# Order of the SP queue and of the last two units in a fused attention and two-MoE kernel

## The chip, the cores and the metric

One core of a Trainium2 chip runs the whole program. The metric is the device time of one execution in microseconds (us). An execution has five compute engines' worth of work: TensorE (PE, with its weight loads as PEld), VectorE (DVE), ScalarE (ACT), GpSimd (POOL), and SyncE (SP), which here only issues transfers. Sixteen DMA engines move the data.

## The reference

```python
x = attention(q, k, v)            # 4 x 8 heads, 576 x 64; a local band of |i-j| < 4, plus
                                  # full attention over means of 4 rows, repeated 4 times
logits = x @ phi                  # x: 2304 x 512; 32 slots, 4 for each of 8 experts
slot_in = softmax(logits, 0).T @ x
slot_out[e] = relu(slot_in[e] @ w1[e]) @ w2[e]          # 512 x 1024, 1024 x 512
x = softmax(logits, 1) @ slot_out
noisy = x @ w_gate + log1p(exp(x @ w_noise)) * noise    # second MoE: top 2 of 8 experts
out[t] += gate * (relu(x[t] @ w1[e]) @ w2[e])           # for the two experts of each row t
```

All is float32. The weights of each MoE are 32 MB.

## The kernel before

The attention is done in 16 units, each two heads of one batch. A unit needs its keys and queries (`load`, L192: four transfers of 144 KB into one of two `ld` buffers) and its values (`load_v`, L213: four transfers of 80 KB into one of three `V` buffers); all of these move in runs of 64 floats. A unit passes through some forty small blocks: A0 and A1 transpose `ld` on PE (`a_pe`, L237), S makes the local scores (`b_s`, L288 and L293), SD the coarse ones (`b_d`, L304), CP and CD turn the probabilities (L379, L390), VD makes the means of the values (`v_pe`, L274), DP and DD multiply with the values (L417, L424), EP transposes the result (L444), LG makes logits (L466), and once per batch SU adds the slots' sums (`slot_u`, L524).

The order is written out by hand. The loop `for p in range(-1, NU - 1)` (L593) walks the string `SEQ` in each step p: a name stands for one block of the unit p minus the block's offset, so a step works on four units at once: `ld` loads unit p+2, A0 and A1 are unit p+1, `lV` loads the values of unit p+1, S is unit p. What is left of the units 13 to 15 after step 14 is the string `TSEQ`, with the unit written beside each block (`S:15`). Nothing reorders it: an engine takes its instructions in the order of the text.

SP issues every load, in the order of the text too. `W` calls `flush`, which issues the next transfers of the first MoE's weights (`wr`, 512 KB each): eight weight matrices are asked for during the attention, one transfer at each `W` of the steps 1 to 12, two at each of the steps 13 and 14. The eight small loads (`small`, L598: the gate's weights and the noise, 16 KB or 4 KB each, in runs of 8 floats) are issued four at a time at the start of the steps 13 and 14. The program gives SP's transfers eight counters in turn, and an issue waits until the transfer that had its counter before has landed, so at most eight are in flight.

`R2` (`ring_2`, L630) gives the attention's buffers up and loads three more weight matrices into their place (`w8a` to `w10b`, 1 MB each), as soon as the last reader of what lay there is done: `w8a` needs unit 15's transposes, `w8b` its S, `w9a` its SD, `w9b` its DP, `w10a` its DD. Five more matrices (`wr`) go into buffers that the first MoE's products give back. The first MoE (L794 to L830) then takes the matrices in this order; its last product is `yacc`, L825.

`cp` (L223) copies a PSUM result to SBUF on ACT, or on DVE where the copy's name stands in `ON_V` (in the tail: `ON_V_END`).

Of the kernel before, what the change touches and what calls it, by code (L numbers as in the profile page):

```python
# [15 lines left out]

CAP = 640

SEQ = """ld DM S DD A0 M a00 a01 A1 W a110 XA a100 SD EL a101 ST a111 SK CP SS EX W VD EP01 MD V0 EP00 EP10 SU_ LG CD
EP11 EP V1 LA ED0 DX SU KD ED1 DP lV x1 x0 DQ1 X0 SE DQ0 RD P0 X1 P1""".split()  # L20
TSEQ = """S:15 DD:13 XA:13 DM:14 CP:14 W EP01:14 EP00:14 SD:15 M:15 EL:15 EP10:14 EX:15 EP11:14 CD:14 ED0:14 MD:15 SU:15 VD:14 DP:14 V0:14 V1:14 EP:13
ED1:14 P0:15 P1:15 DD:14 DX:15 LG:13 X0:13 RD:15 x0:14 DM:15 x1:14 CP:15 LA:13 EP00:15 X1:13 EP01:15 EP11:15
CD:15 EP10:15 XA:14 ED0:15 VD:15 DP:15 V0:15 V1:15 ED1:15 DD:15 EP:14 x0:15 x1:15 LG:14 X0:14 XA:15 LG:15 EP:15 X0:15 LA:14
LA:15 SE:3 X1:14 SK:2 H2 MT M4 X1:15 SS:3 H2 ST:3 MB R2 QW QS UA DN UB H1 SI H2 SK:3""".split()

ON_V = ['k1', 'd1', 'a101', 'a111', 'v0']
ON_V_END = ['P0', 'k1', 'v0', 'v1']

NW = [0] + [1] * 12 + [2] * 2

# [1 line left out]
NPRE = 8  # L32
NHOT = [4, 8]
N2 = 3
# [4 lines left out]
def attn_moe_moe_kernel(ctx: ExitStack, tc: tile.TileContext, q, k, v, moe_phi, moe_w1, moe_w2,  # L39
                        w_gate, w_noise, noise, w1, w2, out, dbg=None):  # L40
    nc = tc.nc
    B, H, S, D = q.shape
    NT = B * S
    DM = H * D
# [11 lines left out]
    NU = len(units)  # L56
# [21 lines left out]
    def consts():  # L78
        nc.vector.tensor_tensor(sums[:, 0], idf[:, 0:32], idf[:, 32:64], op=ALU.add)
        nc.vector.tensor_tensor(sums[:, 0], sums[:, 0], idf[:, 64:96], op=ALU.add)  # L80
        nc.vector.tensor_tensor(sums[:, 0], sums[:, 0], idf[:, 96:128], op=ALU.add)
        nc.vector.tensor_copy(sums[:, 1:4], sums[:, 0:1].to_broadcast([128, 3, 32]))
        nc.vector.tensor_reduce(out=bd, in_=idf.rearrange("p (t s) -> p t s", t=4), axis=AX.X, op=ALU.add)
# [10 lines left out]
    def wload(src, kk, pool=ringa, names=("wr", "wr")):  # L94

        n = kk // 2
        ts = [pool.tile([128, 2048], F32, name=nm).rearrange("p (k f) -> p k f", k=n) for nm in names]
        sv = src.rearrange("(k p) f -> p k f", p=128)

        def go(i, eng=nc.sync, ks=range(n), whole=0):  # L100
            if whole:
                m, k = n // 2, n // 2 * (whole - 1)
                return eng.dma_start(out=ts[i][:, k:k + m], in_=sv[:, n * i + k:n * i + k + m])
            for k in ks:
                eng.dma_start(out=ts[i][:, k:k + 1], in_=sv[:, n * i + k:n * i + k + 1])
        return lambda k: ts[k // n][:, k % n], [lambda i=i, **k: go(i, **k) for i in range(len(names))]
# [12 lines left out]
    with ExitStack() as tctx:  # L119
# [62 lines left out]
        def tp():  # L182
            return ps.tile([128, 512], F32, name="t", bufs=4)

        LD, KD, DQ, SD, SS, SB, PD, PL, XL, XT, XK = ({} for _ in range(11))
# [32 lines left out]
                    if j1 < 5:  # L218
                        nc.sync.dma_start(out=V[64:121, 4, h], in_=hv[h, S - 57:S])

        TAIL = []

        def cp(name, dst, src, alt=False):  # L223
            if name not in (ON_V_END if TAIL else ON_V) and not alt:
                nc.scalar.activation(dst, src, AF.Copy)  # L225
            else:
                nc.vector.tensor_copy(dst, src)
# [13 lines left out]
        def a_evac(u, i, h, j):  # L241
            if i:
                hs = slice(64 * h, 64 * h + 64)
                cp(f"a1{h}{j}", Q[hs, 288 * j:288 * j + 288, h], AT[u, 1, j][hs, 0:288], u == 0)
            else:
                cp(f"a0{j}", K[:, 3 + 288 * j:291 + 288 * j], AT[u, 0, j][:, 0:288])
# [51 lines left out]
        def b_d(u):  # L298
            kd = KD.pop(u)
            sd = ps.tile([128, 512], F32, name="Sd")  # L300
            if u == 1:
                hot(NHOT[1], sd)
            for qb in range(3):
                nc.tensor.matmul(sd[0:96, qb * 144:qb * 144 + 144], Dq[:, qb].rearrange("p h i -> p (h i)"), kd,  # L304
                                 start=True, stop=True, skip_group_check=True)
            SD[u] = sd

        def soft_m(u):
            m = wka.tile([128, NG], F32, name="m")
# [23 lines left out]
        def soft_p(u, a):  # L333
            El, su = PL[u]
            as_ = slice(64 * a, 64 * a + 64)
            eng = nc.vector if f"P{a}" in (ON_V_END if u == NU - 1 else ON_V) else nc.gpsimd
            eng.tensor_tensor(P[as_, :, HQ * a:HQ * a + KW], El[as_],  # L337
# [28 lines left out]
        def soft_dm(u):  # L366
            Ed, rd = PD[u]
            eng = nc.vector if "DM" in (ON_V_END if u == NU - 1 else ON_V) else nc.gpsimd
            eng.tensor_tensor(Ed, Ed, rd[:, :, None].to_broadcast([96, 3, 144]), op=ALU.mult)
# [68 lines left out]
        ET_ = {}  # L438
# [22 lines left out]

        def logit_pe(u):
            xT, kk = XT[u], u % 4
            L = SB[u + 2][:, 0:192] if not TAIL else ET_[u][1][:, 128:320] if u in ET_ else tp()[:, 0:192]
            for t in range(4):
                nc.tensor.matmul(L[32 * t:32 * t + 32, 0:128], phi[:, kk], xT[:, 128 * t:128 * t + 128],  # L466
                                 start=True, stop=True, skip_group_check=True)
            for t in range(4):
                nc.tensor.matmul(L[32 * t:32 * t + 32, 128:192], phi[:, kk], xT[:, 512:576], start=True, stop=True,
                                 skip_group_check=True)  # L470
            LL[u] = L

        def logit_add(u):
            L = LL[u]
            LT = LTs[(u // 4) % 2]
            if u % 4 == 0:
                nc.vector.tensor_copy(LT, L)
            else:
                nc.vector.tensor_tensor(LT, LT, L, op=ALU.add)

# [63 lines left out]
        def hot(n, t=None):  # L544

            t = t or ps.tile([128, 512], F32, name="S")
            for _ in range(n):
                nc.tensor.matmul(t, onesb, onesb[:, None].to_broadcast([128, 4, 128]), start=True, stop=True)

        def ok(u):  # L550
            return 0 <= u < NU
# [21 lines left out]
        MW, todo = {}, []  # L573

        def mload(i, pool, names=("wr", "wr")):
            MW[i], go = wload((moe_w1, moe_w2)[i % 2][i // 2], (4, 8)[i % 2], pool, names)
            if i == 2 * E - 1:
                go = [lambda f=f, c=c: f(ks=(c, c + 2)) for c in range(2) for f in go]
            todo.extend([lambda f=f, c=c: f(whole=c) for f in go for c in (1, 2)] if len(MW) <= NPRE else go)

        def flush(n=99):
            for _ in range(min(n, len(todo))):
                todo.pop(0)()

        for i in range(NPRE):
            mload(ORDW[i], ringa if i < 3 else ringb)
        small = [(wgn[:, :, E * i:E * i + E], w.rearrange("(k p) e -> p k e", p=128))
                 for i, w in enumerate((w_gate, w_noise))]
# [4 lines left out]
        for p in range(-1, NU - 1):  # L593
            if p == 0:
                nc.sync.dma_start(out=phi, in_=moe_phi.rearrange("(k p) s -> p k s", p=128))
            for _ in range(4 if p >= NU - 3 else 0):
                o, i = small.pop(0)
                nc.sync.dma_start(out=o, in_=i)  # L598
            if p == 1:
                nc.gpsimd.memset(zero, 0.0)  # L600
            b4, r4 = divmod(p - 5, 4)
            for nm in SEQ:
                f, off, a = BL.get(nm, (None, 99, ()))
                if off is None:
                    if 0 <= b4 < B and r4 == a:
                        f(b4)
                elif ok(p - off):
                    f(p - off, *a)
                if nm == "W" and p >= 0:
                    flush(NW[p])  # L610
                if p == -1 and nm == "lV":
                    nc.gpsimd.memset(PT, 0.0)
                    nc.gpsimd.memset(Vd[:, 1], 0.0)
                    nc.gpsimd.memset(PdT[:, 1], 0.0)
                if p == -1 and nm == "DQ1":
                    nc.vector.memset(P, 0.0)
            if p == 0:
                hot(NHOT[0])
                nc.vector.tensor_scalar(trib, jp, 0.0, None, op0=ALU.is_gt)
                consts()  # L620
# [47 lines left out]
        def slot_in():  # L668
            t = tp()
            for kk in range(4):  # L670
# [6 lines left out]
              "W": flush}  # L677
        TAIL.append(1)
        for nm in TSEQ:
            if nm in TB:  # L680
                TB[nm]()
            elif nm[0] == "H":
                hot(int(nm[1:]))
            else:
                n, u = nm.split(":")
                f, off, a = BL[n]
                f(int(u), *(a if off is not None else ()))


# [567 lines left out]
    for e in range(E):  # L1257
# [36 lines left out]
        elif nx is not None:  # L1294
# [4 lines left out]
            for n in range(NTILE):  # L1299
                i = s0 + n // 9  # L1300
# [25 lines left out]
        for sl, n0, n1 in SCAT:  # L1326
            if sl // 5 == e:
                f = fill[sl % 5]
# [9 lines left out]
    with tc.If(ov > 0):  # L1338
        with ExitStack() as octx:
# [6 lines left out]
            with tc.For_i(0, E, 1) as ei:  # L1346
# [4 lines left out]
                go = op_.tile([128, NTILE], F32, name="go")  # L1351
# [59 lines left out]
```

## Time and profile before

| | us |
|---|---|
| median of 3 runs (lowest, highest) | 491.67 (491.55, 493.74) |
| the profiled execution | 490.25 |
| its span, first to last instruction | 488.5 |
| PE busy in the span | 462.5 |
| granted clock of TensorE, mean over the span | 0.981 |

The attention with its tail fills the first 158 us, the first MoE goes on to 188 us, the routing to 207 us, and the second MoE's experts take the rest. The page cuts the span in 40 slices; a digit is the busy share of a slice in tenths, for DMA the mean share of its sixteen engines.

### The profile page before, as it was taken

What the parts mean: (1) busy time and instruction counts of PE and PEld (TensorE: products, weight loads), DVE (VectorE), ACT (ScalarE), POOL (GpSimd) and SP (SyncE); (2) the same over time, 40 slices, a digit from 0 to 9 for tenths busy, and PEclk for the clock granted to TensorE, in tenths of its full rate; (3) what the DMA queues carried; (4) which work ended last, traced back from release to release, by engine and by line L of the source; (5) the groups of instructions that cost most, each with busy time, mean ns of one, the idle gap of its engine ahead of it and who ended that gap; (6) DMA issues with size and microseconds to landing.
All of it is one profiled execution on the core that took longest, in us unless ns stands there. A gap on an engine that the chain in (4) does not pass through costs nothing.

```text
span 488.5 us, 12466 instructions
## 1 busy us (share of the span) xinstructions
PE 462.5 (95%) x4765; PEld 358.7 (73%) x4765; DVE 275.3 (56%) x703; ACT 270.5 (55%) x699; POOL 220.1 (45%) x321
## 2 busy tenths in 40 slices
PE   6999999899789999999999999999999999999992
PEld 5798788788575443577777887887887877878882
DVE  6888878878575321876578464383552634615300
ACT  2688877778483112665384464682755646727410
POOL 7898777678331001084556577322222222212232
PEclk9999999999799999979999999999999999999998
DMA  8999999999989999999977843799867855333333
GB/s 163 213 208 257 213 245 216 205 264 186 251 250 333 397 389 395 375 345 335 377 186 203 230 68 67 190 363 280 273 88 214 214 127 144 45 43 45 44 44 46
DMA packets 108233, 104.19 MB, mean 213 GB/s; under 512 B 67978, under 2 KB 77898, under 8 KB 108170
## 3 DMA queue, kind: packets, MB, share of 16 engines
q1 hardware_dynamic: 101258, 90.50, 62.5%
q0 software_dynamic: 6912, 12.85, 17.5%
q8 instruction: 40, 0.66, 0.6%
q14 instruction: 23, 0.19, 0.1%
HBM read 83.60 MB, written 19.73 MB: 212 GB/s over the span
## 4 chain that ended last, share of the span: by engine, by line
PE 58%; DMA 16%; issue 12%; SPq 3%; DVE 3%; ACT 3%; POOL 2%; POOLq 2%; ACTq 0%; DVEq 0%
PE y L1062 35%; DMA wr<-in_moe_w_dram 7%; DMA ld<-in_q_dram 5%; SPq L192 3%; PE t L237 3%; PE gx L879 2%; PE S L293 2%; PE h L1042 2%; PE Sd L304 2%; POOL out_dram L1081 2%; DMA V<-in_v_dram 2%; DMA w10b<-in_moe_w_dram 1%; POOLq L1087 1%; PE gx L1042 1%; PE xs L942 1%
## 5 line engine op out<-in xcount | busy, mean ns | idle before, releaser
L1062 PE MATMUL y<-whi,hh 128*128 128x512 f32 x320 | 127.6, 399 | 0.3 <-ACT hh L1043 0.3
L1062 PE MATMUL y<-whi,hl 128*128 128x512 f32 x320 | 127.7, 399 | 0.0
L1062 PE MATMUL y<-wlo,hh 128*128 128x512 f32 x320 | 127.3, 398 | 0.0
L1081 POOL DMA_INDIRECT out_dram<-ys,idx x40 | 63.9, 1597 | 110.3 <-ACT ys L1073 61.2
L1073 ACT ACTIVATE ys<-y,gt 128x512 f32<-128x512 f32 x40 | 27.4, 685 | 82.4 <-issue 47.1
L1062 PEld LDWEIGHTS y<-wlo,hh 128*128 128x128 f32 x320 | 60.5, 189 | 13.0 <-issue 0.8
L1034 DVE TENSOR_TENSOR wlo<-wr,whi 128x512 fp32r<-128x512 f32 x64 | 42.0, 692 | 49.5 <-ACT whi L1031 38.0
L1062 PEld LDWEIGHTS y<-whi,hh 128*128 128x128 f32 x320 | 60.7, 190 | 12.0 <-ACT hh L1043 0.6
L1062 PEld LDWEIGHTS y<-whi,hl 128*128 128x128 f32 x320 | 60.6, 189 | 11.5 <-issue 2.1
L1008 POOL DMA_INDIRECT tab<-stk,pos x36 | 35.8, 994 | 11.5 <-issue 10.4
L1044 DVE SCALAR_TENSOR_TENSOR hl<-h,hh 128x256 fp32r<-128x256 f32 (+1 forms) x64 | 31.3, 490 | 16.5 <-ACT hh L1043 14.3
L1044 DVE SCALAR_TENSOR_TENSOR hl<-gx,hh 128x256 fp32r<-128x256 f32 (+1 forms) x64 | 31.3, 488 | 11.1 <-ACT hh L1043 8.5
L1031 ACT ACTIVATE whi<-wr 128x512 fp32r<-128x512 f32 x64 | 36.9, 625 | 0.2
L1043 ACT ACTIVATE hh<-gx 128x256 fp32r<-128x256 f32 (+1 forms) x64 | 28.1, 439 | 16.0 <-PE gx L1042 13.2
L1043 ACT ACTIVATE hh<-h 128x256 fp32r<-128x256 f32 (+1 forms) x64 | 27.9, 436 | 13.5 <-PE h L1042 10.7
L237 PE MATMUL t<-idf,ld 96*128 96x96 f32 x192 | 23.5, 271 | 10.8 <-DMA ld<-in_k_dram 7.3
L1080 POOL MEMSET spacer<- 1x1 f32 x40 | 13.6, 339 | 42.4 <-issue 42.4
L255 POOL TENSOR_TENSOR s<-Q 64x288 f32<-64x288 f32 x31 | 29.3, 944 | 2.4
L237 PEld LDWEIGHTS t<-idf,ld 96*128 96x128 f32 x192 | 18.8, 154 | 15.0 <-issue 6.2
L337 POOL TENSOR_TENSOR P<-El,su 64x350 f32<-64x350 f32 x31 | 24.4, 786 | 11.3 <-DVE su L330 5.4
L225 ACT ACTIVATE PT<-t 64x384 f32<-64x384 f32 (+1 forms) x64 | 25.9, 428 | 3.1 <-PE t L379 1.9
L927 DVE TENSOR_TENSOR oh<-iot,R 128x256 fp32r<-128x256 f32 (+2 forms) x50 | 20.7, 447 | 11.5 <-PE xs L945 7.8
(312 smaller groups left out, 882.3 us busy)
## 6 DMA issues: line engine op xcount, KB each, us to landing
wr<-in_moe_w_dram SPq DMA_DIRECT2D x72, 512.0 KB
wr<-in_moe_w_dram SPq DMA_DIRECT2D x88, 256.0 KB
out_dram<-zero SPq DMA_DIRECT2D x20, 256.0 KB
V<-in_v_dram SPq DMA_DIRECT2D x62, 80.0 KB
ld<-in_k_dram SPq DMA_DIRECT2D x32, 144.0 KB
ld<-in_q_dram SPq DMA_DIRECT2D x32, 144.0 KB
XT<-tab SPq DMA_DIRECT2D x5, 320.0 KB
tab<-zero SPq DMA_DIRECT2D x6, 256.0 KB
```

What stands on the lines that cost most here:

```text
L225: nc.scalar.activation(dst, src, AF.Copy)
L237: nc.tensor.transpose(t[:, 96 * c:96 * c + 96], ld[:, i, 3 * j + c].rearrange("p h d -> p (h d)"), idf[0:96, 0:96])
L255: nc.gpsimd.tensor_tensor(q2, q4[:, :, 0:2], q4[:, :, 2:4], op=ALU.add)
L337: eng.tensor_tensor(P[as_, :, HQ * a:HQ * a + KW], El[as_], su[as_, :, None].to_broadcast([64, NG, KW]), op=ALU.mult)
L1008: st = nc.gpsimd.indirect_dma_start(out=tab, out_offset=bass.IndirectOffsetOnAxis(ap=pos[:, c, i:i + 1], axis=0), in_=stk[:, i].bitcast(F3 ...
L1031: nc.scalar.activation(whi[:, kk], wb(kk), AF.Copy)
L1034: eng.tensor_tensor(wlo[:, kk], wb(kk), whi[:, kk].bitcast(F32), op=ALU.subtract)
L1043: nc.scalar.activation(hh[:, f], h, AF.Relu)
L1044: nc.vector.scalar_tensor_tensor(hl[:, f], h, 0.0, hh[:, f].bitcast(F32), op0=ALU.max, op1=ALU.subtract)
L1062: nc.tensor.matmul(y, l[:, kk, ts_], r_[:, kk], start=(m == 0), stop=(m == 23))
L1073: nc.scalar.activation(ys, YS.pop((e, ti)), AF.Copy, scale=gt[:, ti:ti + 1])
L1081: st = nc.gpsimd.indirect_dma_start(out=out, out_offset=bass.IndirectOffsetOnAxis(ap=idx[:, ti:ti + 1], axis=0), in_=ys, in_offset=None, c ...
```

## The change

- `lV` moves from the end of `SEQ` to the place just behind A1, where the first `W` stood; that `W` moves behind CD. So in each step SP is asked for keys and queries, values, weights, in this order; before it was keys and queries, weights, values. At step -1, three clears of POOL (`PT`, `Vd`, `PdT`) move along with `lV`.
- The eight small loads are issued at the end of the steps 13 and 14, not at the start.
- The three matrices of `R2` are loaded in transfers of 512 KB throughout (`<= NPRE + N2`): twelve transfers, before twenty.
- `TSEQ` is another order of the same blocks, and `ON_V_END` is given by unit: five copies change their engine. The logits of the tail are put into the banks of the last S and the last Sd, before into a fresh bank.

```diff
-SEQ = """ld DM S DD A0 M a00 a01 A1 W a110 XA a100 SD EL a101 ST a111 SK CP SS EX W VD EP01 MD V0 EP00 EP10 SU_ LG CD
-EP11 EP V1 LA ED0 DX SU KD ED1 DP lV x1 x0 DQ1 X0 SE DQ0 RD P0 X1 P1""".split()
-TSEQ = """S:15 DD:13 XA:13 DM:14 CP:14 W EP01:14 EP00:14 SD:15 M:15 EL:15 EP10:14 EX:15 EP11:14 CD:14 ED0:14 MD:15 SU:15 VD:14 DP:14 V0:14 V1:14 EP:13
...
+SEQ = """ld DM S DD A0 M a00 a01 A1 lV a110 XA a100 SD EL a101 ST a111 SK CP SS EX W VD EP01 MD V0 EP00 EP10 SU_ LG CD W
+EP11 EP V1 LA ED0 DX SU KD ED1 DP x1 x0 DQ1 X0 SE DQ0 RD P0 X1 P1""".split()
+TSEQ = """DD:13 W S:15 CP:14 SD:15 EP01:14 XA:13 EP11:14 VD:14 M:15 EP00:14 EL:15 EX:15 EP10:14 MD:15 V0:14 V1:14 DM:14 CD:14
...
-ON_V_END = ['P0', 'k1', 'v0', 'v1']
+ON_V_END = ['P0', 'k1:13', 'v0:14', 'p10:15', 'd1:15', 'v0:15', 'x0:15', 'k1:14', 'k1:15']
...
-            L = SB[u + 2][:, 0:192] if not TAIL else ET_[u][1][:, 128:320] if u in ET_ else tp()[:, 0:192]
+            L = (SB[min(u + 2, NU - 1)] if u < NU - 1 else SB["d"])[:, 0:192]
...
-            todo.extend([lambda f=f, c=c: f(whole=c) for f in go for c in (1, 2)] if len(MW) <= NPRE else go)
+            todo.extend([lambda f=f, c=c: f(whole=c) for f in go for c in (1, 2)] if len(MW) <= NPRE + N2 else go)
...
-            for _ in range(4 if p >= NU - 3 else 0):
-                o, i = small.pop(0)
-                nc.sync.dma_start(out=o, in_=i)
             if p == 1:
...
                 if p == -1 and nm == "DQ1":
                     nc.vector.memset(P, 0.0)
+            for _ in range(4 if p >= NU - 3 else 0):
+                o, i = small.pop(0)
+                nc.sync.dma_start(out=o, in_=i)
```

On SP, from the loads of unit 15 (step 13) to the first of the ring's matrices, the program before has these rows; `V_137` are the values of unit 14 and `V_135` those of unit 15.

```order
L598 DMA nz<-in_moe_noise_dram 128x4x8 x2
L192 DMA ld<-in_k_dram 96x6x64 x2
L192 DMA ld<-in_q_dram 96x6x64 x2
L103 DMA wr<-in_moe_w_dram 128x2x512 x4
L213 DMA V_137<-in_v_dram 64x5x64 x4
L598 DMA nz<-in_moe_noise_dram 128x4x8 x2
L598 DMA nz<-in_moe_noise_dram 64x2x8 x2
L103 DMA wr<-in_moe_w_dram 128x1024 x4
L213 DMA V_135<-in_v_dram 64x5x64 x3
L213 DMA V_135<-in_v_dram 64x4x64
L219 DMA V_135<-in_v_dram 57x64
L105 DMA w8a<-in_moe_w_dram 128x512 x4
```

The changed program has these at the same place.

```order
L616 DMA wgn<-in_moe_w_noise_dram 128x4x8
L616 DMA nz<-in_moe_noise_dram 128x4x8 x2
L213 DMA V_135<-in_v_dram 64x5x64 x3
L213 DMA V_135<-in_v_dram 64x4x64
L219 DMA V_135<-in_v_dram 57x64
L103 DMA wr<-in_moe_w_dram 128x1024 x4
L616 DMA nz<-in_moe_noise_dram 128x4x8 x2
L616 DMA nz<-in_moe_noise_dram 64x2x8 x2
L103 DMA w8a<-in_moe_w_dram 128x2x512 x2
```

The small loads have gone from the front of unit 15's keys to the back of the weights of step 13, and the values of unit 15 now stand ahead of the weights of step 14. On PE, the tail before begins with these rows (behind unit 15's scores).

```order
L293 MATMUL S<-K,Q 64x35 x20
L424 MATMUL xb<-PdT,Vd 64x144 x4
L379 MATMUL t<-idf,P 128x128 x5
L304 MATMUL Sd<-kd,Dq 96x144 x3
L390 MATMUL t<-idf,Ed 128x96 x3
L390 MATMUL t<-idf,Ed 16x96 x3
L274 MATMUL xa<-V_137,four 32x128 x8
```

In the changed program it begins with these.

```order
L293 MATMUL S<-K,Q 64x35 x20
L379 MATMUL t<-idf,P 128x128 x5
L304 MATMUL Sd<-kd,Dq 96x144 x3
L274 MATMUL xa<-V_137,four 32x128 x8
L277 MATMUL xb<-V_137,four 32x128
L390 MATMUL t<-idf,Ed 128x96 x3
L390 MATMUL t<-idf,Ed 16x96 x3
```

Unit 13's last product (L424) has moved ahead of unit 15's scores, and the means of unit 14's values ahead of its turned probabilities.

## Rows read from the trace of the kernel before

**Rows 1.** Page, part 2: the span in 40 slices of 12.2 us.

```profile
DMA  8999999999989999999977843799867855333333
```

**Rows 2.** The chain that ended last, 108 to 192 us: start, us, what.

```profile
123.17 3.61 DMA ld<-in_q_dram
...
139.03 7.40 DMA V<-in_v_dram
...
179.59 5.98 DMA wr<-in_moe_w_dram
186.06 0.59 PE yacc L825
```

**Rows 3.** Stretches: busy us of each engine, then TensorE's granted clock, DMA share, GB/s.

```profile
62.00:120.00 58.00, 54.23 (x1095) 46.99 (x1086) 47.14 (x119) 44.55 (x143) 42.25 (x62) 1.00 1.04 231
120.50:122.50 2.00, 2.00 (x83) 1.93 (x82) 1.90 (x7) 2.00 (x10) 1.86 (x4) 1.00 0.23 14
125.50:132.50 7.00, 6.22 (x47) 5.38 (x49) 3.08 (x7) 4.09 (x11) 2.45 (x4) 0.51 1.08 328
133.50:136.50 3.00, 3.00 (x88) 2.48 (x81) 2.60 (x7) 1.75 (x8) 0.63 (x1) 1.00 0.35 41
144.00:150.00 6.00, 3.72 (x80) 2.75 (x78) 1.39 (x5) 3.14 (x9) 0.90 (x2) 1.00 0.69 218
...
156.00:186.00 30.00, 29.71 (x503) 14.24 (x501) 8.35 (x27) 5.71 (x11) 3.59 (x26) 1.00 1.04 393
```

**Rows 4.** SP's issues in order of time: start, us, line, tile, count.

```profile
93.44 2.89 SPq L192 DMA_DIRECT2D ld<-in_q_dram  x2
...
117.56 0.60 SPq L598 DMA_DIRECT2D wgn<-in_moe_w_gate_dram  x1
...
120.06 2.52 SPq L192 DMA_DIRECT2D ld<-in_k_dram  x2
122.62 1.06 SPq L192 DMA_DIRECT2D ld<-in_q_dram  x2
...
129.47 5.22 SPq L598 DMA_DIRECT2D nz<-in_moe_noise_dram  x4
134.73 2.16 SPq L103 DMA_DIRECT2D wr<-in_moe_w_dram  x4
136.99 2.65 SPq L213 DMA_DIRECT2D V<-in_v_dram  x4
```

**Rows 5.** PE in order of time: start, us, line, shapes, count [idle before, releaser].

```profile
89.64 0.69 PE L237 MATMUL t<-idf,ld 96*128 96x96 f32 x6 [0.95 <-DMA ld<-in_k_dram]
...
97.32 0.34 PE L288 MATMUL S<-mask,idb 128*64 128x350 bf16 x2
...
125.27 0.86 PE L237 MATMUL t<-idf,ld 96*128 96x96 f32 x6 [2.06 <-DMA ld<-in_k_dram]
126.91 1.19 PE L237 MATMUL t<-idf,ld 96*128 96x96 f32 x6 [0.78 <-DMA ld<-in_q_dram]
...
136.06 0.34 PE L288 MATMUL S<-mask,idb 128*64 128x350 bf16 x2
...
146.63 0.65 PE L274 MATMUL xa<-V,four 128*32 128x128 f32 x16 [1.21 <-DMA V<-in_v_dram]
```

**Rows 6.** Transfers between 110 and 114 us: SP's queue, packets, MB, share of 16 engines.

```profile
q1 hardware_dynamic: 2753, 0.69, 121.1%
```

**Rows 7.** The same between 133 and 136 us.

```profile
q1 hardware_dynamic: 1552, 0.11, 40.6%
```

**Rows 8.** POOL in order of time, columns as PE's above.

```profile
6.08 0.67 POOL L263 TENSOR_TENSOR s<-K 128x288 f32<-128x288 f32 x1 [2.16 <-ACT K L225]
...
7.19 1.17 POOL L612 MEMSET PT<- 128x1280 f32 x1
```

**Rows 9.** PE's waits between 62 and 120 us: us in total, times, longest.

```profile
PE t L237 <- DMA ld<-in_q_dram: 1.4, 3, 0.5
PE t L237 <- DMA ld<-in_k_dram: 0.9, 1, 0.9
```

More of the change, by code (lines that the diff above doesn't have):

```diff
@@ L17 @@
 CAP = 640
-SEQ = """ld DM S DD A0 M a00 a01 A1 W a110 XA a100 SD EL a101 ST a111 SK CP SS EX W VD EP01 MD V0 EP00 EP10 SU_ LG CD
-EP11 EP V1 LA ED0 DX SU KD ED1 DP lV x1 x0 DQ1 X0 SE DQ0 RD P0 X1 P1""".split()
-TSEQ = """S:15 DD:13 XA:13 DM:14 CP:14 W EP01:14 EP00:14 SD:15 M:15 EL:15 EP10:14 EX:15 EP11:14 CD:14 ED0:14 MD:15 SU:15 VD:14 DP:14 V0:14 V1:14 EP:13
-ED1:14 P0:15 P1:15 DD:14 DX:15 LG:13 X0:13 RD:15 x0:14 DM:15 x1:14 CP:15 LA:13 EP00:15 X1:13 EP01:15 EP11:15
-CD:15 EP10:15 XA:14 ED0:15 VD:15 DP:15 V0:15 V1:15 ED1:15 DD:15 EP:14 x0:15 x1:15 LG:14 X0:14 XA:15 LG:15 EP:15 X0:15 LA:14
-LA:15 SE:3 X1:14 SK:2 H2 MT M4 X1:15 SS:3 H2 ST:3 MB R2 QW QS UA DN UB H1 SI H2 SK:3""".split()
+SEQ = """ld DM S DD A0 M a00 a01 A1 lV a110 XA a100 SD EL a101 ST a111 SK CP SS EX W VD EP01 MD V0 EP00 EP10 SU_ LG CD W
+EP11 EP V1 LA ED0 DX SU KD ED1 DP x1 x0 DQ1 X0 SE DQ0 RD P0 X1 P1""".split()
+TSEQ = """DD:13 W S:15 CP:14 SD:15 EP01:14 XA:13 EP11:14 VD:14 M:15 EP00:14 EL:15 EX:15 EP10:14 MD:15 V0:14 V1:14 DM:14 CD:14
+SU:15 EP:13 DP:14 P0:15 ED0:14 ED1:14 X1:13 DX:15 P1:15 RD:15 DD:14 x0:14 CP:15 x1:14 LG:13 DM:15 X0:13 XA:14 EP11:15
+EP01:15 EP10:15 EP00:15 VD:15 CD:15 V0:15 V1:15 DP:15 ED1:15 ED0:15 LA:13 DD:15 x1:15 LG:14 EP:14 x0:15 XA:15 LG:15
+LA:14 X0:14 LA:15 SE:3 EP:15 X1:14 X1:15 X0:15 SK:2 H2 MT M4 SS:3 H2 ST:3 MB R2 QW QS UA DN UB H1 SI H2 SK:3""".split()
 ON_V = ['k1', 'd1', 'a101', 'a111', 'v0']
-ON_V_END = ['P0', 'k1', 'v0', 'v1']
+ON_V_END = ['P0', 'k1:13', 'v0:14', 'p10:15', 'd1:15', 'v0:15', 'x0:15', 'k1:14', 'k1:15']
 NW = [0] + [1] * 12 + [2] * 2
@@ L219, in load_v @@
                         nc.sync.dma_start(out=V[64:121, 4, h], in_=hv[h, S - 57:S])
-        TAIL = []
+        TAIL, TU = [], [0]
         def cp(name, dst, src, alt=False):
-            if name not in (ON_V_END if TAIL else ON_V) and not alt:
+            if (f"{name}:{TU[0]}" not in ON_V_END if TAIL else name not in ON_V) and not alt:
                 nc.scalar.activation(dst, src, AF.Copy)
@@ L305, in b_d @@
                                  start=True, stop=True, skip_group_check=True)
-            SD[u] = sd
+            SD[u] = SB["d"] = sd
         def soft_m(u):
@@ L686, in attn_moe_moe_kernel @@
                 f, off, a = BL[n]
+                TU[0] = int(u)
                 f(int(u), *(a if off is not None else ()))
```

## The prediction

> **What bounds the kernel now.** I read the page's slices first [rows 1]: the DMA share is at nine tenths in nearly all of the first seventeen slices, which is to 208 us, and low in most that follow. Whatever the first part costs is therefore a question to the sixteen DMA engines, and the change touches only that part. The chain of what ended last [rows 2] says where the first part ends: the last weights of the first MoE were issued at 179.59 and landed 5.98 us later, at 185.57, and the product that needs them (`yacc`) began at 186.06. Everything behind it (routing, experts) is unchanged code that starts from there, and its first weights stand behind these in the same queue. So I count the gain at 185.57.
>
> The stretches [rows 3] then show how full the DMA is on the way. A full queue reads 1.04 here (62 to 120 us, and 156 to 186 us, the latter at 393 GB/s). Three stretches between are not full: 0.23 in 120.5 to 122.5, 0.35 in 133.5 to 136.5, 0.69 in 144 to 150. If the work before 186 us is fixed, only these can be won: 2 x (1 - 0.23/1.04) = 1.6 us, 3 x (1 - 0.35/1.04) = 2.0 us, 6 x (1 - 0.69/1.04) = 2.0 us, in all 5.6 us.
>
> SP's issues [rows 4] say why. The first hole is the four small loads of step 13: their issues take from 117.56 to 120.06, and the next issue, unit 15's keys, takes 2.52 us for two where the two queries behind it take 1.06. So 2.50 + 1.46 = 3.96 us pass before unit 15's loads go out as fast as they can, and the queue runs dry meanwhile. The second hole is the other four: 5.22 us, and only then the weights of step 14. The third is the values of unit 15, which stand behind those weights, and the ring's first matrices behind the values.
>
> PE pays for it too [rows 5], but not at the end. [...] Then it waits 1.21 us for unit 15's values.
>
> **The change part by part.**
>
> *Small loads behind unit 15's keys and the weights.* Unit 15's first transfer can be issued 3.96 us sooner, so its queries land at about 126.78 - 3.96 = 122.8 (now 123.17 + 3.61 = 126.78). PE is ready for them at 125.27 - 2.06 = 123.21. I take an idle time of up to 0.95 us as left, since keys and queries come one after the other; that saves 2.84 - 0.95 = 1.9 us, and the clock should stay. What the half clock costs: from these transposes to the next scores 136.06 - 125.27 = 10.79 us, less 0.78 idle, is 10.0; the same instructions with a slots' sum in them at full clock, four steps earlier, took 97.32 - 89.64 = 7.68, less the 0.5 us that they waited for the queries [rows 9], 7.2. That is 2.8 us. PE gains 4.7 us by the scores of unit 15.
>
> On the DMA the small loads now stand behind 2 MB of weights each time, 2.1 / 393 = 5.3 us of transfer, longer than the 3.96 and not quite disjoint from the 5.22 us that SP needs for them (most of that 5.22 is waiting for the weights before them to land, since eight are in flight). So SP's slowness with them is covered, and the first two holes (3.6 us) close. What does not go away is the small packets' own time. The eight loads are 6 x 512 + 2 x 128 = 3,328 packets of 32 bytes. The trace bounds their price: where they run almost alone, 1,552 packets hold 40.6% of 3 us [rows 7], 0.78 us per 1,000; at most one costs as much as a 256-byte packet in a full queue, 2,753 in 4 us [rows 6], 1.45 us per 1,000. That is 2.6 to 4.8 us for all, and the shares above already count the lower figure as work. In a full queue up to 2.2 us more may show. Nothing speaks for either end, so I take half, 1.1 us.
>
> [...]
>
> *Values asked for before the weights.* In the steps 1 to 13 this turns the order within a step and leaves what stands ahead of the next keys the same: four loads, four values, two weights. The values have a step and more of slack, so they gain nothing. At the end it puts unit 15's values ahead of 2 MB of weights: the 1.21 us go, and PE is 5.9 us ahead. The clears of POOL that move along (1.17 us and two short ones) fall into 2.16 us in which POOL waits for the first keys [rows 8]; without that cover they would cost some 1.7 us once. Nothing.
>
> *Ring in halves.* Eight issues fewer on a queue that waits for landings, not for issues; with eight in flight it now has up to 4 MB under way, before 2 to 3 MB. It helps to close the third hole. I count 1.5 of its 2.0 us, since the matrices there still wait for unit 15's last readers on PE.
>
> *Order of the last units, copies, banks.* None of this moves a byte. It must only keep PE's lead: `w9b` waits for the last product of unit 15 with its values. With PE 5.9 us ahead and the DMA 4 us, that wait is not the later one. Cover is this difference, 1.9 us; beyond it each microsecond that the new order loses on PE costs one.
>
> **Sum.** 1.6 + 2.0 + 1.5 - 1.1 = 4.0 us. Profiled execution: 490.25 - 4.0 = 486.25. The median of the runs stands 1.42 us above that execution, so I forecast 487.7. Its own bounds: without the third hole and with the dear price 3.6 - 2.2 = 1.4 us; all three holes at the cheap price 5.6 us. That is 486.1 to 490.3.
>
> **Rivals.**
>
> *The steady steps gain as well.* Between 62 and 120 us PE waits 1.4 us for queries and 0.9 for keys [rows 9], and queries are now issued behind weights that must land first: the two of 93.44 take 2.89 us where 1.06 do. If the turned order takes that wait from them, 2.3 us come on top: 6.3 us, 485.4. Against it: the share there is 1.04 [rows 3], so loads that come earlier only push other bytes back.
>
> *The cost only moves.* The small loads stall the queue in their new places as in the old ones, so both holes open again between weights and ring, and only the third closes: 0 to 1.5 us, about 490.9. For it: two groups of four have shown the same slowness in two places. Against it: both times there was little in flight behind them, now 2 MB is. [...]
>
> *Slower: the values inherit the queries' wait.* Eight back from the third and fourth value load now stand the weights of the step before. The hold seen at 93.44, 2.89 - 1.06 = 1.8 us, then falls on the values, with two weights and the next unit's keys queued behind on SP. It decides from 4.0 / 7 = 0.6 us of each of the seven steps from unit 9 to 15 that reaches the keys; with half of the hold, 0.9 us, it is 6.4 - 4.0 = 2.4 us slower, 494. Against it: at that point seven other transfers are still in flight, so the engines need not run dry.
>
> **How the numbers follow.** A measurement of this kernel can tell about 0.5%, 2.5 us, from no change. The forecast (486.1 to 490.3, most of it past 2.5 us) gets 0.5, the steady gain 0.15, the cost that only moves 0.25, the slower case 0.1. Faster: most of the first and all of the second, 0.62. Same: the rest of the first, the third, a little of the last, 0.30. Slower 0.08. For eight in ten I leave out the far half of the slower case and a tenth below: 484 to 492.
>
> **What would show it.** Right: PE's idle time before unit 15's transposes under 1 us and the clock at 1.00 through 120 to 140; no stretch between 115 and 185 with a DMA share under 0.9; the last `wr` landing at about 181.5; `yacc` waiting for DMA as now. The first rival shows as fewer waits on queries between 62 and 120 us, with the DMA share the same. The second shows as low shares that have wandered to 128 to 145. The third shows as longer issues of V and waits for keys that grow from unit to unit. The forecast is wrong above all if PE's tail, not the weights, turns out to release the ring last, or if the clock drops at another place.

## The result: the change makes the kernel slower

| | before | after |
|---|---|---|
| median of 20 runs, us | 489.38 (485.10 to 493.74) | 492.69 (489.46 to 497.62) |
| ratio after to before, 95% interval | | 1.007 (1.0046 to 1.0093) |
| profiled execution, us | 490.25 | 497.62 |

The profiled execution of the changed kernel is the slowest of its twenty runs, 4.9 us above their median (those of experiments 9 and 13 below lie 2.8 and 4.0 us above theirs), so its trace shows more than a usual run lost: places and kinds are read from it, sizes from the timed runs.

The page of the changed kernel: DMA share of the 40 slices (now 12.4 us each), then the chain that ended last.

```profile
DMA  8998999899869999999987844599947856333333
...
PE 72%; issue 10%; DVE 6%; DMA 5%; ACT 2%; POOL 2%; POOLq 2%; SPq 0%; DVEq 0%; ACTq 0%
```

The chain in the page of before:

```profile
PE 58%; DMA 16%; issue 12%; SPq 3%; DVE 3%; ACT 3%; POOL 2%; POOLq 2%; ACTq 0%; DVEq 0%
```

Beside [rows 1] the slices look alike but for the twelfth (136 to 149 us, now 6), and the chain has changed hands: 72% of it is PE and 5% DMA. [rows 2] ran through the loads. The last weights now land later:

```profile
180.71 6.58 DMA wr<-in_moe_w_dram
187.31 6.04 DMA wr<-in_moe_w_dram
```

That is 193.35 us where it was 185.57; 181.5 was forecast. The stretches, columns as in [rows 3], with one more at the end:

```profile
62.00:120.00 58.00, 52.35 (x991) 45.19 (x981) 42.45 (x110) 40.25 (x129) 37.09 (x55) 0.94 1.00 217
120.50:122.50 2.00, 2.00 (x76) 1.93 (x68) 1.61 (x6) 1.71 (x7) 1.92 (x3) 1.00 0.80 200
125.50:132.50 7.00, 6.57 (x149) 5.90 (x142) 6.60 (x19) 6.61 (x24) 5.65 (x8) 1.00 0.77 158
133.50:136.50 3.00, 3.00 (x58) 1.87 (x54) 2.77 (x7) 2.24 (x7) 1.19 (x2) 1.00 0.98 296
144.00:150.00 6.00, 6.00 (x125) 4.88 (x123) 4.37 (x13) 5.67 (x19) 2.17 (x3) 1.00 0.86 270
...
24.00:118.00 94.00, 87.76 (x1725) 75.98 (x1721) 70.89 (x184) 70.07 (x227) 67.50 (x99) 0.96 0.98 217
```

The half clock of before at 125.5 to 132.5 is gone, as forecast (0.51 in [rows 3], 1.00 now). At the old places of the three holes the share has risen (0.80, 0.98, 0.86), but this trace runs some 5 us late there, and the low shares have moved with it:

```profile
130.00:132.00 2.00, 1.57 (x18) 1.34 (x15) 1.84 (x6) 1.86 (x8) 1.43 (x2) 1.00 0.41 80
140.00:146.00 6.00, 5.20 (x74) 4.75 (x74) 2.17 (x7) 1.82 (x6) 0.45 (x1) 0.72 0.40 89
```

The first stands behind the values of unit 14, the second behind small loads and the values of unit 15, which SP issues ahead of the next weights:

```profile
134.29 2.98 SPq L616 DMA_DIRECT2D nz<-in_moe_noise_dram  x2
137.38 6.17 SPq L213 DMA_DIRECT2D V<-in_v_dram  x4
...
144.12 2.91 SPq L103 DMA_DIRECT2D wr<-in_moe_w_dram  x4
```

The larger loss stands earlier: 62 to 120 us, which read 1.04 and 231 GB/s, moved 217 GB/s, at a granted clock of 0.94. SP's issues there, columns as in [rows 4]:

```profile
78.03 5.33 SPq L213 DMA_DIRECT2D V<-in_v_dram  x4
83.41 1.08 SPq L103 DMA_DIRECT2D wr<-in_moe_w_dram  x2
84.59 1.06 SPq L192 DMA_DIRECT2D ld<-in_k_dram  x2
85.70 1.43 SPq L192 DMA_DIRECT2D ld<-in_q_dram  x2
87.23 6.19 SPq L213 DMA_DIRECT2D V<-in_v_dram  x4
```

A step of before, in the same columns:

```profile
78.73 0.99 SPq L103 DMA_DIRECT2D wr<-in_moe_w_dram  x2
79.82 2.81 SPq L213 DMA_DIRECT2D V<-in_v_dram  x4
82.72 3.17 SPq L192 DMA_DIRECT2D ld<-in_k_dram  x2
```

Four value loads take 5.3 and 6.2 us where they took 2.65 to 3.5 in the steps of before. Over the ten full steps from 24 to 118 us the first of each four takes 1.84 us on average (0.60 before), the third and fourth 0.9 (0.6 and 0.7), while the second key load has become shorter (1.62 before, 0.61 now). SP is held in both kernels, at one or more issues of a step (a step's ten issues take 8.0 us before, 8.3 now); what has changed most is where.

A step as a whole has become longer. The first key loads of unit 4 and of unit 14 stand ten steps apart; in before 87.5 us:

```profile
21.62 1.10 SPq L192 DMA_DIRECT2D ld<-in_k_dram  x2
...
109.12 1.95 SPq L192 DMA_DIRECT2D ld<-in_k_dram  x2
```

In the changed kernel it is 91.6 us:

```profile
20.81 0.94 SPq L192 DMA_DIRECT2D ld<-in_k_dram  x2
...
112.41 0.98 SPq L192 DMA_DIRECT2D ld<-in_k_dram  x2
```

PE's waits from 62 to 120 us, as in [rows 9]:

```profile
PE S L293 <- issue: 4.4, 3, 2.0
PE xb L417 <- issue: 1.0, 1, 1.0
PE t L237 <- DVE xT L436: 0.3, 1, 0.3
```

No wait for keys or queries is left. In their place PE stops with no releaser at all. One of these, in PE's order of time:

```profile
72.45 1.07 PE L293 MATMUL S<-K,Q 128*64 128x35 f32 x30
75.24 0.57 PE L293 MATMUL S<-K,Q 128*64 128x35 f32 x10 [1.72 <-issue]
```

It stops 1.72 us in the middle of forty equal products, after thirty. In the DMA view of 72.4 to 74.0 us, one transfer of 16 KB in the queue of kind `instruction` stands beside 1,186 packets of data:

```profile
q1 hardware_dynamic: 1186, 0.29, 123.5%
q8 instruction: 1, 0.02, 5.2%
```

By its record it ended at 73.86, and PE went on 1.38 us later. I counted PE's instruction records in order of time: this stop stands at number 2497, which is 193 modulo 256. Six more of over 0.3 us stand at 193 modulo 256 before 185 us (the view puts one of them down to ScalarE), and none without a releaser stands elsewhere. They sum to 8.2 us; before had one, 0.5 us. All seven ended 1.3 to 1.9 us after a 16 KB transfer of that queue had ended, and before's one 1.6 us after. That PE waited there for late pieces of its program is my reading; the trace shows places and times only.

### The profile page after: what moved, and what is told of

It reads as the page before. It is cut to its first block, busy times and chain, and to the rows that moved or that the text cites. A ratio compares the mean times of both kernels' runs of the same rounds, so it can differ in the third digit from the quotient of the medians.

```text
span 495.8 us, 12443 instructions
## 1 busy us (share of the span) xinstructions
PE 465.5 (94%) x4765; PEld 362.0 (73%) x4765; DVE 277.1 (56%) x704; ACT 269.6 (54%) x698; POOL 220.6 (44%) x321
## 4 chain that ended last, share of the span: by engine, by line
PE 72%; issue 10%; DVE 6%; DMA 5%; ACT 2%; POOL 2%; POOLq 2%; SPq 0%; DVEq 0%; ACTq 0%
PE y L1063 34%; PE S L293 4%; PE t L237 3%; PE yacc L826 3%; DMA wr<-in_moe_w_dram 3%; PE gx L880 2%; PE hp L802 2%; PE Sd L304 2%; PE t L390 2%; PE xb L424 2%; PE xa L417 2%; PE t L379 2%; PE xa L274 2%; PE h L1043 2%; POOL out_dram L1082 2%
## 5 line engine op out<-in xcount | busy, mean ns | idle before, releaser
L1044 ACT ACTIVATE hh<-gx 128x256 fp32r<-128x256 f32 (+1 forms) x64 | 28.1, 439 | 16.1 <-PE gx L1043 14.2
L1081 POOL MEMSET spacer<- 1x1 f32 x40 | 13.6, 341 | 39.4 <-issue 39.4
L293 PE MATMUL S<-K,Q 128*64 128x35 f32 x640 | 23.8, 234 | 6.2 <-issue 4.4
L293 PEld LDWEIGHTS S<-K,Q 128*64 128x64 f32 x640 | 23.7, 149 | 7.1 <-issue 7.0
```

Source lines behind the costliest of these rows:

```text
L293: nc.tensor.matmul(s[64 * a:64 * a + 64, KW * g:KW * g + KW], Q[:, c0:c0 + 32].rearrange("p i h -> p (i h)"), K[:, c0:c0 + KW], start=Fals ...
L1044: nc.scalar.activation(hh[:, f], h, AF.Relu)
```

## The experiments

Each is timed in five rounds beside the kernel before on the same chip; ratios are to that, with a 95% interval. Two rival theories stood first: **Q**, that the order keys, values, weights costs time in the queue, and **T**, that the tail's order does; **S** is the start.

**1. The order alone**, in the program before:

```diff
-... A1 W a110 ... LG CD EP11 ... DP lV x1 ...
+... A1 lV a110 ... LG CD W EP11 ... DP x1 ...
```

> The program before with one change: values are asked for behind the keys and ahead of the weights in each step (the string SEQ), with POOL's three clears left in their old place. Theory Q (the queue: the early values hold SP, its issues of V take 1 to 3 us where they took 0.6, weights and the next keys stand behind them): slower than before by 3 us or more, 492 to 494, with the long V issues in the trace. Theory T (the new order of the last units costs PE time, the queue is neutral as forecast): as before, 488.5 to 490.5, V issues near 0.6 us.

Measured: 495.72, ratio 1.0129 (1.0079 to 1.0178). **2. The same undone** in the changed program:

> The changed program with SEQ alone put back (values behind the weights, at the end of a step; the clears go back with them). Theory Q: the loss goes and what the small loads and the ring give is left, 485 to 488. Theory T: the loss stays, 491 to 494. Theory S (the start: POOL's clears slow VectorE, PE's first scores begin 1.9 us later) alone: 490.5 to 491.5.

Measured: 487.23, ratio 0.9950 (0.9925 to 0.9975). T falls, Q stands: the order costs 1.2 to 1.3%, about 6 us, and what is left of the change gains 2.4 us. This kernel beats both. PE's rows in it where it waits, from 120 us:

```profile
120.91 0.69 PE L237 MATMUL t<-idf,ld 96*128 96x96 f32 x6 [0.42 <-DMA ld<-in_k_dram]
122.45 0.69 PE L237 MATMUL t<-idf,ld 96*128 96x96 f32 x6 [0.85 <-DMA ld<-in_q_dram]
...
140.88 0.38 PE L274 MATMUL xa<-V,four 128*32 128x128 f32 x5 [2.47 <-DMA V<-in_v_dram]
...
181.53 0.62 PE L826 MATMUL yacc<-wr,hz 128*32 128x512 f32 x1 [0.25 <-DMA wr<-in_moe_w_dram]
```

**3. The clears.** In the changed kernel one of VectorE's first operations had grown. In its order of time, before:

```profile
3.17 0.93 DVE L167 TENSOR_SCALAR fa<-fi 128x288 f32<-128x288 f32 x1
```

after:

```profile
3.17 2.46 DVE L167 TENSOR_SCALAR fa<-fi 128x288 f32<-128x288 f32 x1
```

And POOL's three clears stand in the gap of [rows 8]:

```profile
3.88 1.16 POOL L609 MEMSET PT<- 128x1280 f32 x1
4.98 0.19 POOL L610 MEMSET Vd<- 128x128 f32 x1
5.13 0.33 POOL L611 MEMSET PdT<- 128x288 f32 x1
```

POOL's last clear ends at 5.46 and VectorE's operation at 5.63. With the clears put back behind DP:

```diff
-                if p == -1 and nm == "lV":
+                if p == -1 and nm == "DP":
```

> The changed program with only POOL's three clears of step -1 put back to their old place, behind DP; everything else, the early values too, stays. Theory S (start): PE's first scores begin at 7.6 us again and 1.9 us come off, 490 to 491. Theories Q and T: the first scores begin sooner, but what is lost later takes it up again, 492 to 494.

Measured: 494.62, ratio 1.0073 (1.0036 to 1.0110). The operation takes 0.93 again and PE's first scores begin at 8.02, not 9.48; the time doesn't follow. S falls: what PE loses at the start does not show in the time.

**4, 10, 12. The parts without the order**, each in the program before (their diffs are in the change): small loads and ring; tail; small loads.

> The program before with the small loads moved behind the steps 13 and 14 and the ring in halves, nothing else. The forecast's own sum for these (first two holes 3.6, third 1.5, less 1.1 for small packets, less 0.5 for the values of unit 15 that now stay behind the weights): 3.5 us faster, 485 to 487, no half clock between 120 and 140. Rival (the small loads stall the queue wherever they stand): 488.5 to 490.

> The program before with only the new order of the last two units, their copies by unit and the logits' banks. The forecast: costs nothing and brings nothing, 488.5 to 490.5. Theory T (the new order lengthens PE's path to the ring): 491 or more. If it lets PE give the ring up sooner: 487 to 488.5.

> The program before with only the small loads moved to the end of the steps 13 and 14. The forecast's terms for this edit (the first two holes close, 3.6 us, less 1.1 for their packets in a full queue): 2.5 us faster, 487 to 488, first keys of unit 15 in time and no half clock at 125 to 132. Rival (they hold the queue in the new place as in the old): 489 to 491.

Measured: small loads and ring 488.86, 0.9979 (0.9946 to 1.0011); tail 489.76, 0.9996 (0.9964 to 1.0029); small loads alone 488.71, 0.9954 (0.9922 to 0.9986). The small loads bring 2.3 us (0.7 to 3.8), the tail nothing, the ring nothing that can be told.

The holes have moved, not closed. In experiment 12 unit 15's keys are in time and the clock is 1.00 from 120 to 140 us, but behind each four of the small loads stands a hole. One of SP's issues, then the stretches:

```profile
139.71 4.75 SPq L616 DMA_DIRECT2D nz<-in_moe_noise_dram  x4
```

```profile
132.00:134.00 2.00, 2.00 (x78) 1.78 (x78) 1.87 (x6) 1.95 (x9) 1.25 (x2) 1.00 0.48 41
142.00:146.00 4.00, 2.32 (x47) 1.70 (x46) 0.00 (x0) 1.20 (x4) 0.00 (x0) 0.69 0.24 24
```

The half clock comes later as well: 6.8 us from 143.5 (in experiments 2 and 4 for 3.4 and 6.8 us, from 142.5 and 143.0). Counted from the packet records, idle is the share of the sixteen DMA engines with no packet under way, summed over time: from 118 to 165 us it is 6.7 us in before, 5.6 in experiment 12 and 6.1 in experiment 4. So the rival that the small loads stall the queue in the new place too is right about the holes; its time, 489 to 491, begins just above the 488.71 measured. Where the 2.3 us come from is not shown.

**5, 6, 7. PE's stops.** They could have been the cause and not a by-product. Tiny products that nobody reads, ahead of everything, put 64 or 128 instructions more ahead of PE's code:

```diff
                 t = tp()
+                for _ in range(32 if u == i == j == 0 else 0):
+                    nc.tensor.matmul(t[:, 0:8], onesb, onesb[:, 0:8], start=True, stop=True, skip_group_check=True)
```

> The changed program with 32 tiny matmuls on PE ahead of everything (8 columns each, overwritten at once, in the 4 us in which PE waits for the first keys): 64 instructions more on PE, so that the stops of PE with no releaser, which all stand at one place modulo 256 instructions, should come 64 instructions earlier in the code. Theory F (PE stops because a piece of its own program arrives late, and how often that is depends on where the pieces begin against SP's bursts): the stops come 64 instructions earlier in the code and the time moves by 2 us or more, either way. Theory Q (SP's long V issues starve the engines, the stops are a by-product): 492 to 495, as the changed program.

> The same with 64 tiny matmuls, 128 instructions. Theory F: yet other places and another time than with 64 instructions, between 487 (few stops) and 497. Theory Q: 492 to 496 (PE begins up to 1 us later).

> The program before with the same 32 tiny matmuls. Theory F: the program before had its pieces at lucky places (one stop of 0.5 us in its profile) and loses 1 to 4 us with others, 490 to 494. Theory Q: as before, 488.5 to 490.5.

Measured: changed kernel with 64 and 128 instructions more 492.73, 1.0060 (1.0028 to 1.0092), and 494.20, 1.0071 (1.0038 to 1.0105); before with 64 more 488.94, 0.9972 (0.9938 to 1.0007). The stops do move with the code, still at 193 modulo 256, and their sum falls from 8.2 to 3.1 and 4.2 us. The time doesn't. With 64 more, PE waits from 24 to 118 us so:

```profile
PE t L239 <- DMA ld<-in_k_dram: 3.4, 3, 2.1
PE t L239 <- DMA ld<-in_q_dram: 2.3, 3, 1.4
PE Sd L306 <- issue: 0.5, 1, 0.5
```

In that stretch it waits 5.7 us for keys and queries, 0.4 in the changed kernel's trace. F falls: the sum of the stops fell by 5.1 and 4.0 us, the time by nothing that can be told.

**9. One weight between keys and values.**

```diff
-... A1 lV a110 ... EX W VD ... LG CD W EP11
+... A1 W lV a110 ... EX W VD ... LG CD EP11
```

> The changed program with one of each step's two weight transfers put between the keys and the values (keys and queries, weights, values, weights). Between 24 and 118 us the engines stood idle for 14 to 16 us in all five runs with the new order and for 4 to 9 us in the five with the old one. Theory R (refill: SP is held once in each step, and what it issues right behind the hold must take longer to move than to issue; values don't): idle 6 to 11 us there, 488.5 to 491. Rival (any weight behind the values costs the whole, since the third and fourth value load wait for weights eight back): idle 13 us or more, 492 to 494.

Measured: 492.32, ratio 1.0038 (1.0007 to 1.0070), idle 8.7 us. The idle time fell as R said; that the time came down from the changed kernel's 1.007 is not clear of the noise.

**13. A fourth value buffer**, so that PE can't be what holds SP:

```diff
-            V = Vs[u % 3]
+            V = Vs[u % 4]
```

> The changed program with four V buffers instead of three, so that the values of a unit wait for the last reader of the unit four before, which was done a step (7.4 us) earlier. Theory B (what holds SP for 2 us at the first value load is PE, the last reader of the buffer): the hold shrinks to 0.6 us, the DMA share of 24 to 118 us rises from 0.94-0.98 to 1.03 or more, 487 to 490. Theory R (SP is held by the queue itself, and the values behind the hold can't refill it): hold and share as in the changed program, 492 to 495.

Measured: 492.35, ratio 1.0037 (0.9999 to 1.0075), idle 14.6 us. One of SP's issues, then the stretch of the table below:

```profile
88.49 5.22 SPq L213 DMA_DIRECT2D V<-in_v_dram  x4
```

```profile
24.00:118.00 94.00, 87.84 (x1727) 76.23 (x1723) 71.75 (x184) 70.10 (x225) 67.95 (x98) 0.96 0.96 216
```

The hold is no shorter (2.0 us on the first value load, mean of ten steps, against 1.84). B falls: it isn't PE that holds SP at this buffer.

**14. A weight behind the keys.**

```diff
             for i, src in enumerate((k, q)):
+                if i and u >= 3:
+                    flush(NW[u - 2])
```

> The changed program with the old SEQ, and the first weight transfer of each step put between its keys and its queries: keys, weight, queries, weight, values. In the old order SP's hold falls on the second key load (1.4 us where 0.5 will do), and the engines stand idle while SP issues the queries behind it. Theory R: a transfer that takes longer to move than to issue now comes right behind the hold, so the share of 24 to 118 us is 1.10 or more, idle below the 4.7 us of the run with the old SEQ, 484 to 487. If the queries then come late to PE: the share as there, waits on queries of 3 us or more, 488 to 491.

Measured: 496.66, ratio 1.0135 (1.0083 to 1.0188), idle 6.6 us. The stretch, then PE's waits in it:

```profile
24.00:118.00 94.00, 83.39 (x1559) 72.04 (x1558) 67.39 (x172) 64.58 (x207) 62.51 (x91) 0.93 1.07 209
```

```profile
PE S L295 <- issue: 4.7, 2, 3.0
PE t L239 <- DMA ld<-in_q_dram: 4.2, 3, 2.2
```

R's time fails: the engines are busy, the queries come late to PE, and the busy share moves less (209 GB/s at 1.07, against 235 at 1.10 in experiment 2). In the packet records a 2 KB packet takes 130 ns here, 116 in experiment 9 and 93 to 109 in the other fourteen kernels. Why they are slower in this order is not shown.

**8, 11. Towards a better version.** From experiment 2: unit 15's values ahead of the weights in step 14 alone; and the small loads at the end of the steps 0 and 1.

```diff
+                if nm == "W" and p == NU - 2:
+                    load_v(NU - 1)
```

```diff
-            for _ in range(4 if p >= NU - 3 else 0):
+            for _ in range(4 if p in (0, 1) else 0):
```

> The changed program with the old SEQ, but in the last step (14) alone the values of unit 15 are asked for ahead of the weights. The wait of 2.5 us for them, which the run with the old order still shows, and the half clock of 3.4 us behind it go: 485.5 to 487.5, 0.3% under that run; if the weights alone set the end there, as that run, 487 to 488.

> The changed program with the old SEQ and the eight small loads at the end of the steps 0 and 1, where the first 23 us show 5 us of idle engines and no weights are asked for yet. If the small loads cost their own packets (2.6 to 4.8 us) wherever the queue is full: 1 to 3 us under the run with the old SEQ, 485 to 487. If they only push the first units back: 488 to 490.

Measured: 488.04, 0.9963 (0.9933 to 0.9993), and 489.35, 0.9977 (0.9945 to 1.0010). Neither beats experiment 2. In the first, PE still waits 3.86 us for those values. In the second, the ten steps from unit 4 to 14 take 85.3 us, in experiment 2 85.0, but begin 5.8 us later (27.27 and 21.45): the small loads push the first units back, as its second case had it.

All sixteen kernels from 24 to 118 us, from that row of the stretches of each, and the time of the ten steps from unit 4's first key load to unit 14's, from SP's issues:

| order in a step | kernels | DMA share | GB/s | ten steps, us | ratio |
|---|---|---|---|---|---|
| keys, weights, values | before, 2, 4, 7, 8, 10, 11, 12 | 1.03 to 1.10 | 223 to 235 | 85.0 to 88.4 | 0.9950 to 1 |
| keys, weight, values, weight | 9 | 1.04 | 211 | 94.3 | 1.0038 |
| keys, values, weights | after, 1, 3, 5, 6, 13 | 0.94 to 0.98 | 212 to 218 | 91.6 to 94.0 | 1.0037 to 1.0129 |
| keys, weight, queries, weight, values | 14 | 1.07 | 209 | 95.3 | 1.0135 |

In the first group the engines are idle 3.9 to 9.4 us there, in the third 14.2 to 16.4.

## Why the prediction was wrong

**The step that failed** is "In the steps 1 to 13 this turns the order within a step and leaves what stands ahead of the next keys the same", and with it the cost of nothing. The four, four and two transfers are the same; the order is not neutral. It costs 1.2 to 1.3%, some 6 us, against a forecast gain of 4.0. The rows show it: ten steps of SP take 92.6 us on average in the six kernels with the new order and 86.3 in the eight with the old one.

Everything else together gained 2.4 us by the timed runs (experiment 2). That the profiled execution of experiment 2 is 486.19 us, the forecast 486.25, and its `yacc` began at 181.53, forecast about 181.5, is luck: 2.5 of the 4.1 us that this execution gained stand in the ten steps (85.0 us against 87.5), whose order there is that of before.

By the terms of the sum:
- *Small loads, 3.6 less 1.1*: the size fits, 2.3 us measured for 2.5, but the mechanism failed, so the fit is luck. "SP's slowness with them is covered, and the first two holes (3.6 us) close" is not what experiment 12 shows: behind the weights the second four still take SP 4.75 us (5.22 before), and the share falls to 0.48 and 0.24 behind them. What came true stands ahead of that: PE's idle time before unit 15's transposes is 0.42 and 0.85 us in experiment 2, 0.90 in experiment 12 and 0.43 in the changed kernel, there at one of the seven stops, and the clock stays at 1.00 through that place in all three.
- *Third hole and ring, 1.5*: not seen; small loads and ring together gained no more than the small loads alone (intervals overlap widely).
- *Unit 15's values*: in the changed kernel PE no longer waits for them, as forecast. But PE was not 5.9 us ahead: its last scores began at 140.80, 4.7 us later than the 136.06 of [rows 5], after what it had lost in the steps.
- *Clears*: "without that cover they would cost some 1.7 us once" was about POOL's idle time. POOL was covered; VectorE's `fa` took 2.46 us for 0.93, and PE's scores came 1.9 us later (9.48, 7.59 before). It shows in no timed run.
- *Order of the last units, nothing*: right, 0.9996.
- *The clock*: the half clock is gone at 125.5 to 132.5. In the changed kernel the clock went down to half for 3.4 us at 75.5, 113.0 and 140.3, each time within 1.1 us of the end of a stop of PE of 1.7 to 2.0 us; the stop of 0.95 us at 83.29 left it at 1.00. That it would stay at 1.00 after up to 0.95 us was an estimate from one row (0.95 us idle at 89.64 in [rows 5], the stretch at 1.00 in [rows 3]); nothing here shows how long an idle time brings it down.

**The bound.** "The work before 186 us is fixed, only these can be won" let me look for holes in the profile of before and not for holes that the change could make. Nor was the share of 1.04 full: by the packet records the engines of before are idle for 9.2 us between 24 and 118 us, at a share of 1.03, and experiment 2 reaches 1.10 there with 4.7. A new order at 0.98 is a loss over a hundred microseconds.

**The rivals.** The slower one, at 0.1, named the right edit, the longer value issues and the sign, and gave 494. Its mechanism is not shown: the hold falls on the first value load, not on the third and fourth, which grew by 0.3 us each; and keys came late to PE in experiment 5, not in the changed kernel's trace, where stops without a releaser (8.2 us) stood instead. That the steady steps gain was wrong by sign, though the waits of [rows 9] did go. "The cost only moves" (0.25) had its sign: low shares at 130 to 132 and 140 to 146 us in the changed kernel, at 132 to 134 and 142 to 146 in experiment 12. Its price, 0 to 1.5 us of gain, can't be told from the 0.7 to 3.8 of experiment 12.

**What is shown and what not.** Shown: the order of the queue costs the time (1 against 2), and it costs it over the steady steps (the table: 6.3 us on average over ten of them, with no overlap between the two orders). Neither the clears, nor the tail, nor the place of PE's stops carry it. That the value buffers do not is shown by the hold, the idle time and the ten steps (92.6 us); the interval of the time alone reaches from nothing to the whole loss.

Argued: why. Summed by what SP issues meanwhile, 13.6 of the 14.3 idle us of the changed kernel fall on the third and fourth value load, the weights and the keys, so behind the hold. A value load brings 80 KB per issue of 0.60 us, 137 GB/s, below the 229 that the stretch moves; a weight brings 512 KB in 0.5. On this estimate three value loads refill the queue slowly behind a hold; queries and weights, which stood there before, do it fast. Against it: experiment 9 agrees in the idle time (8.7 us) and not in the time, since its ten steps are no faster and its ratio is that of experiment 13, whose idle time is 14.6; 14 does not agree either, and within the old order idle times of 3.9 and 9.4 us go with ratios of 0.9972 and 0.9954. So the idle time alone is not the price. What holds SP at the second key load before and at the first value load now, with some 2,000 to 2,600 small packets issued and not yet moved (those of the held issue among them), stays open; the last reader of the value buffer is excluded.

## What to carry to other kernels

In a queue that is full, an order is not neutral merely because its bytes and counts are the same: try it alone, as one line of the change can cost more than the rest gains (here some 6 us against 2.4). Read a transfer by its issue time as well as by its bytes (the first value load took 0.60 us in one order and 1.84 in the other), and see what is issued behind a place where the issuing engine is held. Look at the rate of a stretch when waits vanish from an engine's list: here 2.3 us of waits for keys and queries went, 5.4 us of stops came, and the rate fell from 231 to 217 GB/s.

## What the runs showed of the hardware

- In the traces of before and of the changed kernel the queue of kind `instruction` (q8) moved 40 transfers of 16 KB, beside the data. In sixteen kernels PE stopped 50 times for over 0.3 us (up to 3.0) at record 193 modulo 256 before 185 us, each time until 1.3 to 1.9 us after the end of such a transfer (in before once, in the changed kernel seven times). What ties the two is not shown.
- VectorE's `fa` operation began at 3.17 in both kernels and ended 0.17 us after POOL's memsets then running (4.10 after 3.93, 5.63 after 5.46). It took 0.93 us before and 2.46 with the three clears (3.88 to 5.46) behind those memsets, and 0.93 again in experiment 3, with the clears put back. Why is not shown.
- A DMA share of 1.07 went with 209 GB/s (experiment 14), one of 1.10 with 235 (experiment 2): here the share alone didn't tell how fast the work went. Nor did a share over 1 mean that no engine was idle: in before 9.2 of 94 us were, at 1.03.
